# A first dense layer by seven block products for a pair of batches, in runs that use all PSUM banks

## The chip, the cores and the metric

The kernel runs on one core of one Trainium2 chip. The metric is device time in microseconds (us) of one execution; the time before is the median of three runs. A profile is one execution with the hardware profiler on; its span is the time from its first to its last instruction.

The engines: TensorE (PE) multiplies matrices and accumulates into the eight PSUM banks of 512 fp32 columns; PEld is its loading of weights, which overlaps matmuls. ScalarE (ACT) applies functions, VectorE (DVE) does arithmetic on whole tiles, GpSimd (POOL) and SyncE (SP) here only issue DMAs. Each engine works through its own queue in order and waits on semaphores for the others.

## The reference

There are 8 batches of 12 heads, 448 tokens and 64 dimensions a head, then a gated layer of width 2048:

```python
scores = q @ k.T / sqrt(64) - log(448)
attn = sigmoid(scores) @ v                  # per batch and head
x = attn, heads side by side                # 3584 tokens x 768
h = x @ w_in                                # 768 x 2048, first layer
g = h * sigmoid(beta * h)
out = g @ w_out                             # 2048 x 768, second layer
```

The kernel computes in fp16 with fp32 accumulation.

## The kernel before, in words

Four heads make a "quad" `g` (three quads a batch, 24 in all), two heads a slot. A **visit** (`visit`, L222) works on one quad and one chunk `jt` of 128 keys (the last chunk has 64, and is done for two quads at once): eight score matmuls of 448 columns with 32 rows each, four of which run side by side in TensorE (`score`, L201), into two score tiles of two PSUM banks each. ScalarE then makes a sigmoid of each tile (`weigh`, L212, 128x896). `attend` (L267) multiplies a quad's weights with the values, 16 matmuls of which at least two run side by side, into two banks; VectorE casts the result into `xT`, the first layer's input (L276).

The first layer (`dense1`, L285) is done by column blocks `dc` of 128 of the 2048: six matmuls of 128x128 by 448 columns into one bank (192 of half width for batch 0), then ScalarE's sigmoid (L293) and VectorE's product (L296) into `gt`. `gt` holds two batches, a window of seven tiles of 128 tokens.

The second layer multiplies tiles of `gt` by `w_out`. Tiles 0, 1, 2 and 27 are done plainly (`dense2`, L315: 32 matmuls of 384 columns, or the like in other widths). The 24 tiles between are done in pairs by seven block products in place of eight (`strassen`, L397: 7 x 8 matmuls of 384 columns for two tiles). Its sums of `gt` (`hidden_sum`, L386) and of `w_out` (`weight_sum`, L361, once) and its additions of results (L416, L419, L421) are done by VectorE, with one copy by ScalarE.

PSUM's eight banks are split: after the early stage two score tiles take four banks, and the other four (`bank`) serve values, first and second layer in turn, the one that was used longest ago first; a bank whose sum is still open is held (`held`).

The order of work is written out by the kernel. The first and second layer are units in a list (`filler_stream`, L467); after each visit the loop at L594 issues as many units as a budget in estimated us allows, so that TensorE has matmuls while ScalarE makes the sigmoids. A batch's first layer thus lies between visits of the next batches, unit by unit (`dense1` of six matmuls, `strassen` of four). What is left after the last visit (some 16 first-layer units and the last second-layer tiles) runs at the end. Queries, keys and values are loaded by POOL (L111, L132, L139), results are stored by SP (L450).

Of the kernel before, what the change touches and what calls it, by code (L numbers as in the profile page):

```python
# [13 lines left out]
def kernel(  # L14
# [27 lines left out]
    NHC = DM // P  # L42
    NDC = DFF // P
# [12 lines left out]
    qTp = ctx.enter_context(tc.tile_pool(name="qTp", bufs=4))  # L56
    kTp = ctx.enter_context(tc.tile_pool(name="kTp", bufs=4))
    attnp = ctx.enter_context(tc.tile_pool(name="attnp", bufs=12))
# [3 lines left out]
    outp = ctx.enter_context(tc.tile_pool(name="outp", bufs=4))  # L62
    psum = {}
    used = {}
    held = {}

    def share_psum(pools: ExitStack, n_sc: int, n_one: int):
        for name, bufs in (("sc", n_sc), ("one", 1)):
            psum[name] = pools.enter_context(
                tc.tile_pool(  # L70
                    name=f"ps_{name}{n_sc}",
                    bufs=bufs,
                    space=bass.MemoryType.PSUM,
                    reuse_waits="tile",
                )
            )
        used.clear()
        used.update((i, i - n_one) for i in range(n_one))
# [4 lines left out]

    def bank(name: str, cols: int = S, hold=None):
        i = min((i for i in used if i not in held.values()), key=used.get)
        touch(i)
        if hold is not None:
            held[hold] = i
        return psum["one"].tile([P, cols], FP32, tag=f"one{i}", name=name)

# [5 lines left out]
    w_in16 = const.tile([P, NHC, DFF], FP16, name="w_in16")  # L96
    w_out16 = const.tile([P, NDC, DM], FP16, name="w_out16")

# [66 lines left out]


# [25 lines left out]
    def score_tile():  # L195
        return psum["sc"].tile([P, 2, 512], FP32, tag="sco", name="sco")
# [13 lines left out]
    def weigh(sco, n: int):  # L210
        at = attnp.tile([P, 2, S], FP16, tag="attnT", name="attnT")
        nc.scalar.activation(  # L212
            out=at[:, :, 0:n],
            in_=sco[:, :, 0:n],
            func=AF.Sigmoid,
            bias=nlogs[:, 0:1],
            scale=MSCALE,
        )
        return at


    def visit(g: int, jt: int, also=()):  # L222
        if jt < JF:
            todo = [(score_tile(), [s]) for s in (2 * g, 2 * g + 1)]
        else:
            todo = [(score_tile(), [2 * h, 2 * h + 1]) for h in (g, *also)]
        for e in range(PAIR):
            for sco, slots in todo:
                for s in slots:
                    for hh in range(2):  # L230
                        score(sco, 0, s, jt, hh, e, 0, S)
        for sco, slots in todo:
            at = weigh(sco, S)
            for s in slots:
                at_tiles[s, jt, 0] = at


    def half_visit(g: int, c0: int, second: int):
# [14 lines left out]
        for s, jt, sco, u0 in plan:  # L253
            at_tiles[s, jt, c0] = ats[id(sco)][:, :, u0 : u0 + QH]

    def attend(g: int, c0: int, n: int, part=(0, 1)):
# [4 lines left out]
        avs = [bank("av_ps") for _ in slots]  # L261
        todo = [(s, av, jt) for s, av in zip(slots, avs) for jt in range(JF)]
        for s, av, jt in todo + [(s, av, JF) for s, av in zip(slots, avs)]:
            at = at_tiles.pop((s, jt, c0))
# [16 lines left out]
    def dense1(b: int, dc: int, c0: int = 0, n: int = S):  # L281
        off = (b % 2) * S + c0
        m1 = bank("m1_ps")
        for hc in range(NHC):
            nc.tensor.matmul(  # L285
                m1[:, 0:n],
                w_in16[:, hc, dc * P : (dc + 1) * P],
                xTs[b][:, hc, c0 : c0 + n],
                start=(hc == 0),
                stop=(hc == NHC - 1),  # L290
            )
        sg = sigp.tile([P, S], FP32, tag="sg", name="sg")
        nc.scalar.activation(  # L293
            out=sg[:, 0:n], in_=m1[:, 0:n], func=AF.Sigmoid, bias=0.0, scale=beta_sb[:, dc : dc + 1]
        )
        nc.vector.tensor_tensor(  # L296
            out=gt[:, dc, off : off + n], in0=m1[:, 0:n], in1=sg[:, 0:n], op=ALU.mult
# [3 lines left out]
    N2 = 4  # L301

# [4 lines left out]
    def dense2(t: int, half: int, part: int):  # L307
        last = t == NT - 1
        mid = 512 if last else HALF
        lo, hi = (0, mid) if half == 0 else (mid, DM)  # L310
        if part == 0:
            m2s[t, half] = bank("m2_ps", hi - lo, (t, half))
        m2 = m2s[t, half]
        for dc in range(part * NDC // N2, (part + 1) * NDC // N2):
            nc.tensor.matmul(  # L315
                m2,
                gt[:, dc, cols(t)],
                w_out16[:, dc, lo:hi],
                start=(dc == 0),
                stop=(dc == NDC - 1),  # L320
            )
        if part < N2 - 1:
            return
        release((t, half))
        if half == 0:
            osbs[t] = outp.tile([P, DM], FP32, tag="osb", name="osb")
        osb = osbs[t]
        nc.vector.tensor_copy(out=osb[:, lo:hi], in_=m2)  # L328
        if last:
            store(t, lo, hi)  # L330
        elif half == 1:
            store(t, 0, DM)

    NT = NTOK // P

    def cols(t: int):
        return slice(t % NTILE * P, (t % NTILE + 1) * P)

# [8 lines left out]
    ws = {  # L347
        name: const.tile([P, ND, HALF], FP16, name=f"w_{name}")
        for name in ("T1", "T3", "T4", "T6", "T7")
    }  # L350

    def weight_sum(name: str, part: int):
# [8 lines left out]
        nc.vector.tensor_tensor(out=ws[name][:, rows], in0=x[:, rows], in1=y[:, rows], op=op)  # L361

# [25 lines left out]
    def strassen(t: int, i: int, part: int):  # L388
        name, x, _, op, w = product(t, i)
        if part == 0 and i + 2 < NPROD:  # L390
            hidden_sum(t, i + 2)
        first = (t, name) not in m2s
        if first:
            m2s[t, name] = bank("m2_ps", HALF, (t, name))
        m2 = m2s[t, name]
        for dc in range(part * ND // 2, (part + 1) * ND // 2):
            nc.tensor.matmul(  # L397
                m2,
                (x if op is None else sums[t, i])[:, dc],
                w[:, dc],  # L400
                start=first and dc == 0,
                stop=(dc == ND - 1),
                skip_group_check=i >= 4,
            )
            first = False if dc else first
        if part == 0:
# [46 lines left out]
    M1_US, M1H_US, M2_US, LEAST_US = 1.13, 0.58, 2.6, 2.0  # L453


    def second_layer(tiles):
        for t in tiles:
            if t < 3 or t == NT - 1:
                for half in range(2):
                    for part in range(N2):  # L460
                        yield M2_US / N2, lambda a=(t, half, part): dense2(*a), False
            elif t % 2:
                for i in range(NPROD):
                    for part in range(2):
                        yield M2_US / 4, lambda a=(t, i, part): strassen(*a), i in (2, 3) or (i, part) == (4, 0)

    def filler_stream():  # L467
        for c0 in (0, QH):
            for dc in range(NDC):
                if c0 and dc == 10:  # L470
                    for part in range(N2):
                        yield M2_US / N2, 0, lambda part=part: dense2(0, 0, part), False
                yield M1H_US, 0, lambda dc=dc, c0=c0: dense1(0, dc, c0, QH), False
        for t, half in ((1, 0), (2, 0), (0, 1), (1, 1), (2, 1)):
            for part in range(N2):
                yield M2_US / N2, 0, lambda a=(t, half, part): dense2(*a), False
        for b in range(1, B):
            for dc in range(NDC):
                yield M1_US, QPB * (b + 1), lambda b=b, dc=dc: dense1(b, dc), False
            ends = [((x * S // P) - 1) // 2 * 2 + 1 for x in (b, b + 1)]  # L480
            for cost, unit, opens in second_layer(range(ends[0], NT if b == B - 1 else ends[1])):
                yield cost, 0, unit, opens

    fill = list(filler_stream())
    at_fill = [0]

    def fill_units(n: int):
        for _ in range(n):
            fill[at_fill[0]][2]()
# [3 lines left out]
    firsts = ctx.enter_context(ExitStack())  # L493
    share_psum(firsts, 3, 2)
    with tc.manual_schedule():
# [9 lines left out]
        idle = bank("idle_ps", 512)  # L505
# [49 lines left out]
        firsts.close()  # L555
        share_psum(ctx, 2, 4)
        fill_units(4)
        half_visit(1, QH, 1)
        attend(0, QH, QH)
        fill_units(3)  # L560
        half_visit(2, QH, 0)
        fill_units(4)
        half_visit(2, QH, 1)
        attend(1, QH, QH)
        fill_units(4)
        transpose(QPB, 0)
        fill_units(1)
        attend(QPB - 1, QH, QH)
        transpose(QPB, 1)
        fill_units(4)  # L570

        visits = [(QPB, jt, ()) for jt in range(JF + 1)]
        for g in range(QPB + 1, NQUAD, 2):
            visits += [(g, jt, ()) for jt in range(JF)] + [(g, JF, (g + 1,))]
            visits += [(g + 1, jt, ()) for jt in range(JF)]
        spread = [3 * M1H_US, 3 * M1H_US + M2_US / 2, M2_US / 2 + 3 * M1H_US, 3 * M1H_US]
        spread += [5 * M2_US / 7] * 7
        spread += [2.95] * (sum(g < 4 * QPB for g, _, _ in visits) - len(spread))

        total = sum(u[0] for u in fill[at_fill[0] :])  # L580
        tail = 16 * M1_US + 9.6 * M2_US
        rest = (total - sum(spread) - tail) / (len(visits) - len(spread))
        adds = {
            5: [("T4", 0)],
            6: [("T4", 1)],
            8: [("T3", 0)],
            9: [("T3", 1), ("T1", 0)],
            10: [("T1", 1), ("T6", 0)],
            11: [("T6", 1)],
            12: [("T7", 0)],  # L590
            13: [("T7", 1)],
        }
        budget, spent = 0.0, 0.0
        for i, (g, jt, also) in enumerate(visits):  # L594
            if jt == 0:
                if g > QPB:


# [62 lines left out]
```

## Time and profile before

| | before |
|---|---|
| median of 3 runs | 388.36 us (387.67 to 388.69) |
| span of the profiled execution | 386.3 us |
| TensorE busy | 98% of the span, 2991 matmuls |
| ScalarE busy, VectorE busy | 63%, 59% |
| granted TensorE clock | full in all 40 slices |
| first-layer matmuls of 448 columns (L285) | 672, 134.2 us |
| first-layer matmuls of 224 columns (L285) | 192, 20.3 us |
| second-layer matmuls by block products (L397) | 672, 119.5 us |
| sigmoids of scores (L212, 896 columns) | 165, 157.1 us |
| ScalarE idle, waiting for scores | 80.7 us |

The run's time is longer than the profiled span by about 2 us. Busy time of an engine is the union of its instructions' spans; a matmul's span (353 ns for 448 columns) is longer than the distance to the next one's start, since they are pipelined. A wait is put down to the instruction that ended last before it.

### The profile page before, as it was taken

Reading aid. Unit: us, or ns where it says so; the run is one execution under the profiler, and the core shown is the slowest. Engines: PE = TensorE matmul, PEld = TensorE weight load, DVE = VectorE, ACT = ScalarE, POOL = GpSimd, SP = SyncE. Lnnn points to the kernel's source line nnn. Section 1 sums busy time; section 2 is a strip of 40 time slices with the busy share of each in tenths; the row PEclk is TensorE's granted clock in tenths of the full one; section 3 lists DMA queues with packets and bytes.
Section 4 is the critical chain, followed back from the end, with each engine's and each line's share of the span. In section 5 each row is a group of like instructions: output and inputs, shape, how many; then the busy total and the mean of one; then the engine's idle time right before and its main releaser. Section 6 shows DMA issues by size and latency. Waiting matters only on the chain.

```text
span 386.3 us, 7378 instructions
## 1 busy us (share of the span) xinstructions
PE 379.8 (98%) x2991; PEld 191.4 (50%) x2991; DVE 229.5 (59%) x437; ACT 242.0 (63%) x329; POOL 67.4 (17%) x117
## 2 busy tenths in 40 slices
PE   8989999999999999999999999999999999999996
PEld 3468754444554444444554445544455444555563
DVE  3356465784766557555765566655586565645762
ACT  4987966687384795597375783567762777625200
POOL 8833433131110410140110410104100000000000
PEclk9999999999999999999999999999999999999999
DMA  8999999828352850655363561639203300030033
GB/s 119 180 195 203 198 204 197 174 38 88 49 119 68 127 68 0 130 69 52 49 129 79 83 73 20 129 78 125 41 9 83 83 1 2 0 83 0 2 81 122
DMA packets 42401, 34.30 MB, mean 89 GB/s; under 512 B 21872, under 2 KB 38784, under 8 KB 42368
## 3 DMA queue, kind: packets, MB, share of 16 engines
q0 software_dynamic: 36976, 22.81, 43.1%
q1 hardware_dynamic: 5392, 11.02, 11.1%
q8 instruction: 23, 0.38, 0.4%
q14 instruction: 10, 0.08, 0.1%
HBM read 45.62 MB, written 11.01 MB: 147 GB/s over the span
## 4 chain that ended last, share of the span: by engine, by line
PE 97%; ACT 1%; DVE 1%; issue 0%
PE m_ps L285 39%; PE m_ps L397 29%; PE sco L201 12%; PE av_ps L267 9%; PE m_ps L315 6%; PE idle_ps L509 2%; ACT attnT L212 1%; DVE qT L179 0%; ACT sg L293 0%; DVE gt L296 0%; DVE kT L187 0%; DVE osb L328 0%; DVE xT L276 0%; DVE still L503 0%
## 5 line engine op out<-in xcount | busy, mean ns | idle before, releaser
L212 ACT ACTIVATE attnT<-sco,nlogs 128x896 f16<-128x896 f32 (+1 forms) x171 | 160.3, 991 | 81.3 <-PE sco L201 80.7
L285 PE MATMUL m_ps<-xT,w_in 128*128 128x448 f16 (+1 forms) x864 | 154.5, 332 | 1.3 <-ACT attnT L212 1.2
L296 DVE TENSOR_TENSOR gt<-m_ps,sg 128x448 f16<-128x448 f32 (+1 forms) x144 | 80.0, 572 | 84.2 <-ACT sg L293 84.2
L285 PEld LDWEIGHTS <-w_in 128*128 128x128 f16 x864 | 80.8, 98 | 71.7 <-issue 16.6
L293 ACT ACTIVATE sg<-m_ps,beta_sb 128x448 f32<-128x448 f32 (+1 forms) x144 | 82.3, 595 | 32.0 <-PE m_ps L285 29.9
L397 PEld LDWEIGHTS <-sum 128*128 128x128 f16 x480 | 45.2, 98 | 36.4 <-issue 7.9
L201 PE MATMUL sco<-qT,kT 32*128 32x448 f16 (+3 forms) x864 | 51.9, 340 | 1.0 <-ACT attnT L212 0.6
L397 PE MATMUL m_ps<-w_T,sum 128*128 128x384 f16 x288 | 51.6, 327 | 0.0
L111 POOL DMA_DIRECT2D raw<-in_q_dram x27 | 14.9, 553 | 189.9 <-DVE kT L191 183.5
L416 DVE TENSOR_TENSOR osb<-m_ps,osb 128x384 f32<-128x384 f32 x60 | 33.3, 555 | 18.7 <-PE m_ps L397 16.9
L267 PE MATMUL av_ps<-attnT,v 128*64 128x448 f16 (+3 forms) x432 | 41.3, 340 | 0.0
L276 DVE CAST xT<-av_ps 128x448 f16<-128x448 f32 (+1 forms) x54 | 28.6, 567 | 19.0 <-PE av_ps L267 19.0
L386 DVE TENSOR_TENSOR sum<-gt 128x1024 f16<-128x1024 f16 x60 | 39.1, 678 | 0.1
L397 PE MATMUL m_ps<-w_T,gt 128*128 128x384 f16 x192 | 34.2, 326 | 0.0
L397 PE MATMUL m_ps<-w_out,sum 128*128 128x384 f16 x192 | 33.7, 326 | 0.0
L267 PEld LDWEIGHTS <-v 128*64 128x64 f16 (+1 forms) x432 | 18.9, 107 | 23.8 <-issue 16.1
L201 PEld LDWEIGHTS <-kT 32*128 32x128 f16 (+1 forms) x864 | 13.4, 96 | 28.6 <-issue 25.9
L397 PEld LDWEIGHTS <-gt 128*128 128x128 f16 x192 | 18.1, 98 | 14.7 <-issue 3.1
L315 PE MATMUL m_ps<-w_out,gt 128*128 128x384 f16 (+2 forms) x128 | 22.5, 327 | 0.0
L132 POOL DMA_DIRECT2D v<-in_v_dram x32 | 19.8, 641 | 7.6 <-DMA w_in<-in_moe_w_in_dram 5.8
L179 DVE STREAM_TRANSPOSE qT<-raw 128x448 f32<-128x448 f32 (+1 forms) x27 | 16.5, 616 | 3.7 <-DMA raw<-in_q_dram 3.7
L315 PEld LDWEIGHTS <-gt 128*128 128x128 f16 x128 | 11.9, 98 | 10.3 <-issue 3.1
(24 smaller groups left out, 97.0 us busy)
## 6 DMA issues: line engine op xcount, KB each, us to landing
out_dram<-osb SPq DMA_DIRECT2D x98, 96.0 KB, 1.9
raw<-in_k_dram POOLq DMA_DIRECT2D x24, 224.0 KB, 4.5
raw<-in_q_dram POOLq DMA_DIRECT2D x21, 224.0 KB, 3.7
v<-in_v_dram POOLq DMA_DIRECT2D x32, 144.0 KB, 6.1
w_in<-in_moe_w_in_dram POOLq DMA_DIRECT2D x8, 384.0 KB, 10.4
w_out<-in_moe_w_out_dram POOLq DMA_DIRECT2D x4, 768.0 KB, 14.0
v<-in_v_dram POOLq DMA_DIRECT2D x16, 48.0 KB, 6.1
out_dram<-osb SPq DMA_DIRECT2D x2, 384.0 KB, 2.3
```

Source lines behind the costliest of these rows:

```text
L132: nc.gpsimd.dma_start(out=vs[b][i * BLK : (i + 1) * BLK, :, 0:JF].rearrange("p h j d -> p h (j d)"), in_=rows[:, :, JF * i * D : JF * (i + ...
L201: nc.tensor.matmul(sco[base : base + nk, hh, u0 : u0 + n], kT[g][lo : lo + BLK, jt * P : jt * P + nk, e], qT[g][lo : lo + BLK, c0 : c0 + n ...
L212: nc.scalar.activation(out=at[:, :, 0:n], in_=sco[:, :, 0:n], func=AF.Sigmoid, bias=nlogs[:, 0:1], scale=MSCALE,)
L267: nc.tensor.matmul(av[hh * D : (hh + 1) * D, 0:n], vs[b][base : base + nk, 2 * (s % NPAIR) + hh, jt], at[base : base + nk, hh, 0:n], start ...
L276: nc.vector.tensor_copy(out=xTs[b][:, s % NPAIR, c0 : c0 + n], in_=av[:, 0:n])
L285: nc.tensor.matmul(m1[:, 0:n], w_in16[:, hc, dc * P : (dc + 1) * P], xTs[b][:, hc, c0 : c0 + n], start=(hc == 0), stop=(hc == NHC - 1),)
L293: nc.scalar.activation(out=sg[:, 0:n], in_=m1[:, 0:n], func=AF.Sigmoid, bias=0.0, scale=beta_sb[:, dc : dc + 1])
L296: nc.vector.tensor_tensor(out=gt[:, dc, off : off + n], in0=m1[:, 0:n], in1=sg[:, 0:n], op=ALU.mult)
L315: nc.tensor.matmul(m2, gt[:, dc, cols(t)], w_out16[:, dc, lo:hi], start=(dc == 0), stop=(dc == NDC - 1),)
L386: nc.vector.tensor_tensor(out=sums[t, i], in0=x, in1=y, op=op)
L397: nc.tensor.matmul(m2, (x if op is None else sums[t, i])[:, dc], w[:, dc], start=first and dc == 0, stop=(dc == ND - 1), skip_group_check= ...
L416: nc.vector.tensor_tensor(out=out, in0=in0, in1=in1, op=op)
```

## The change

The first layer of batches 2 to 7 is done for two batches at once. With the 768 inputs and the 2048 outputs cut in halves, the 2x2 blocks of `w_in` and the two batches' halves of `xT` make seven products with sums of blocks (Winograd's form) in place of eight. Sums of `w_in` (`in_sum`) are made once, differences of `xT` (`x_sums`) for each pair. The second layer's window of two batches has seven tiles: three pairs, and one tile by itself (`single`, with the same number of matmuls as a plain tile). Two sums of `w_out` and one of `w_in` now overwrite their operands.

These first layers run without attention between: `first_layer` closes the values that are due, gives up the score tiles so that `bank` has all eight banks, and calls `blocks`. A run has eight blocks and makes 168 matmuls; at its two ends it issues four second-layer matmuls three times (`other`). Partial results are carried in PSUM and in free slots of the attention weights' buffer (`scratch`). Runs stand after the first visit of quads 12 and 18 and after the last one. Between them lie visits, values and second-layer matmuls, now in units of one matmul, paced by what is left over the visits that are left. Values come after the first scores of the next quad, not ahead of them.

PSUM is one tile with banks by index, the attention weights one buffer of 14 slots; `qT`, `kT` have three buffers for four, the output tiles three for four.

```diff
-    qTp = ctx.enter_context(tc.tile_pool(name="qTp", bufs=4))
-    kTp = ctx.enter_context(tc.tile_pool(name="kTp", bufs=4))
-    attnp = ctx.enter_context(tc.tile_pool(name="attnp", bufs=12))
+    qTp = ctx.enter_context(tc.tile_pool(name="qTp", bufs=3))
+    kTp = ctx.enter_context(tc.tile_pool(name="kTp", bufs=3))
...
-    outp = ctx.enter_context(tc.tile_pool(name="outp", bufs=4))
+    outp = ctx.enter_context(tc.tile_pool(name="outp", bufs=3))
...
+    ps = psp.tile([P, 8, 512], FP32, name="ps")
...
+    def share_psum(sc: int, first: bool = False):
+
+        age = min(used.values()) - 1 if first else max(used.values())
+        while len(scored) > sc:
+            used.update((i, age) for i in scored.pop())
+        while len(scored) < sc:
+            free = [i for i in used if i not in held.values()]
+            scored.append(
+                min(
+                    ((i, i + 1) for i in free if i + 1 in free),
+                    key=lambda two: sorted((used[i] for i in two), reverse=True),
                 )
             )
...
+    def single(t: int, n: int, dc: int):
+
+        if (n, dc) == (0, 0):
+            sums[t, 0] = sump.tile([P, ND, P], FP16, tag="sum", name="sum")
+            nc.vector.tensor_tensor(out=sums[t, 0], in0=hid(t, 0), in1=hid(t, 1), op=ALU.add)
...
+        half, x, w = (
+            (1, hid(t, 0), B12),
+            (0, hid(t, 1), B21),
+            (1, both, B22),
+            (0, both, B11),
+        )[n]
...
+    def in_sum(name: str, part: int):
+        x, y, op = {
+            "S3": (A11, A21, ALU.subtract),
+            "S1": (A21, A22, ALU.add),
+            "S2": (A22, us["S3"], ALU.subtract),
+            "S4": (A12, us["S2"], ALU.subtract),
+        }[name]
...
+        yield lambda: minus(t1[:, c], y[:, c], x[:, c])
+        yield lambda: minus(t2[:, c], y[:, d], t1[:, c])
+        yield lambda: minus(t3[:, c], y[:, d], y[:, c])
+        yield lambda: minus(t4[:, c], x[:, d], t2[:, c])
+
+    def product1(b: int, i: int, n: int, out, start: bool):
+
+        x, y = xTs[b], xTs[b + 1]
+        t1, t2, t3, t4 = xs[b]
+        w, m = (
+            (A11, x[:, 0:KH]),
+            (A12, x[:, KH:]),
+            (us["S4"], y[:, KH:]),
+            (A22, t4),
+            (us["S1"], t1),
+            (us["S2"], t2),
+            (us["S3"], t3),
+        )[n - 1]
+        for c in range(KH):
+            nc.tensor.matmul(
+                out,
+                w[:, c, i * P : (i + 1) * P],
+                m[:, c],
+                start=(start and c == 0),
+                stop=(c == KH - 1),
+                skip_group_check=not start,
+            )
+
+    def gate(h, dc: int, b: int):
+        sg = sigp.tile([P, S], FP32, tag="sg", name="sg")
+        nc.scalar.activation(
+            out=sg, in_=h, func=AF.Sigmoid, bias=0.0, scale=beta_sb[:, dc : dc + 1]
+        )
+        return lambda: nc.vector.tensor_tensor(
+            out=gt[:, dc, b % 2 * S : b % 2 * S + S], in0=h, in1=sg, op=ALU.mult
+        )
+
+    def blocks(b: int, other):
+
+        kept = {}
+
+        def whole(key, i):
+            h = kept.pop((i, key))
+            if (i, key) in held:
+                touch(held.pop((i, key)))
+            half, second = {"A": (0, 0), "D": (0, 1), "B": (1, 0), "E": (1, 1)}[key]
+            return gate(h, i + half * NB1, b + second)
+
+        for i in range(NB1 + 1):
+            p5 = scratch(6 + i % 2, 1).bitcast(FP32)
+            if i < NB1:
+                B = kept[i, "B"] = bank(S, (i, "B"))
+                product1(b, i, 1, B, True)
+                A = kept[i, "A"] = bank(S, (i, "A"), S)
+                nc.scalar.copy(out=A, in_=B)
+                D = kept[i, "D"] = bank(S, (i, "D"))
+                product1(b, i, 5, D, True)
+                nc.scalar.copy(out=p5, in_=D)
+            if i:
+                product1(b, i - 1, 3, kept[i - 1, "D"], False)
+                late = whole("E", i - 1)
+            else:
+                other()
+            if i < NB1:
+                product1(b, i, 6, B, False)
+                nc.vector.tensor_tensor(out=D, in0=B, in1=p5, op=ALU.add)
+            if i:
+                late()
+                whole("D", i - 1)()
+            if i < NB1:
+                product1(b, i, 2, A, False)
+                whole("A", i)()
+            if i in (0, NB1):
+                other()
+            if i:
+                product1(b, i - 1, 4, kept[i - 1, "B"], False)
+            if i < NB1:
+                product1(b, i, 7, B, False)
+                E = kept[i, "E"] = scratch(8 + i % 2, 1).bitcast(FP32)
+                nc.vector.tensor_tensor(out=E, in0=B, in1=p5, op=ALU.add)
+            if i:
+                whole("B", i - 1)()
...
+    M1_US, M2_US = 0.148, 0.164
...
+    def window(w: int):
+        yield from pairs(w * NTILE, 3)
+        yield from alone((w + 1) * NTILE - 1)
...
+        AV_US = 1.3
...
+        def first_layer(b: int):
+            while due:
+                values(due.pop())
+            while soon:
+                soon.pop(0)()
+            fill_units(len(fill) - at_fill[0] - ND)
+            share_psum(0, True)
+            fill.extend(window(b // 2))
+            blocks(b, lambda: fill_units(ND // 2))
...
+            if n in turn_at:
+                first_layer(turn_at[n])
+                share_psum(2)
...
+            todo = left_us(L1B) if g < 2 * QPB else left_us(len(fill)) - (2.0 if g < 6 * QPB else 4.0)
+            pace = (todo + phase["values"] * AV_US) / phase["visits"]
+            phase["visits"] -= 1
+            owed = pace
+            if jt == 0 and g > QPB:
+                due.append(g - 1)
+            while due or (at_fill[0] < len(fill) and fill[at_fill[0]][0] / 2 < owed):
+                if due and (jt >= 1 or clear()):
+                    values(due.pop())
+                elif fill[at_fill[0]][0] / 2 < owed:
+                    spend()
+                else:
+                    break
...
+        due.append(NQUAD - 1)
+        first_layer(B - 2)
         fill_units(len(fill) - at_fill[0])
```

## The prediction

> **What bounds the kernel now.** I read the page's busy table, then its clock row, then the waits, the groups by shape, and a stretch of the timeline in the middle.
>
> ```profile
> PE 379.8 (98%) x2991; PEld 191.4 (50%) x2991; DVE 229.5 (59%) x437; ACT 242.0 (63%) x329; POOL 67.4 (17%) x117
> PEclk9999999999999999999999999999999999999999
> ```
>
> ```profile
> 105.00:340.00 235.00, 235.00 (x1774) 111.43 (x1770) 144.52 (x264) 154.02 (x201) 27.57 (x48) 1.00 0.40 67
> ```
>
> The second fence is the windows view: length, then PE, PEld, DVE, ACT, POOL busy, then the granted clock. From 105 to 340 us TensorE is never idle and its clock is full. So the time is the sum of TensorE's matmuls, and only a shorter sum, or a new wait of TensorE, moves it.
>
> ```profile
> PE m_ps L285 <- ACT attnT L212: 1.2, 1, 1.2
> PE sco L201 <- ACT attnT L212: 0.6, 2, 0.3
> ```
>
> These waits (us, times, longest) are nearly all that TensorE spends on other engines: no wait is left to remove, and any that the change adds is lost in full. Next, what the followers of a matmul cost (groups by shape; between the bars stand the busy us and the mean ns of one, behind them the idle time before):
>
> ```profile
> L212 ACT ACTIVATE attnT<-sco,nlogs 128x896 f16<-128x896 f32 x165 | 157.1, 1004 | 81.3 <-PE sco L201 80.7
> L293 ACT ACTIVATE sg<-m_ps,beta_sb 128x448 f32<-128x448 f32 x112 | 68.8, 635 | 28.3 <-PE m_ps L285 28.3
> L296 DVE TENSOR_TENSOR gt<-m_ps,sg 128x448 f16<-128x448 f32 x112 | 67.9, 624 | 72.0 <-ACT sg L293 72.0
> L419 ACT COPY osb<-m_ps 128x384 f32<-128x384 f32 x12 | 5.7, 478 | 15.5 <-PE m_ps L397 15.5
> ```
>
> And the rhythm of one score visit (timeline, TensorE's and ScalarE's own rows):
>
> ```profile
> 191.77 0.57 PE L201 MATMUL sco<-qT,kT 32*128 32x448 f16 x8
> 192.28 2.12 PE L397 MATMUL m_ps<-w_T,sum 128*128 128x384 f16 x12
> 194.34 0.57 PE L201 MATMUL sco<-qT,kT 32*128 32x448 f16 x8
> ```
>
> ```profile
> 192.38 1.90 ACT L212 ACTIVATE attnT<-sco,nlogs 128x896 f16<-128x896 f32 x2 [4.84 <-PE sco L201]
> 194.95 1.91 ACT L212 ACTIVATE attnT<-sco,nlogs 128x896 f16<-128x896 f32 x2 [0.66 <-PE sco L201]
> ```
>
> Scores start at 191.77, ScalarE starts 0.61 later and is done 2.51 after them. TensorE's next scores come at 2.57 (0.60 for the scores with both changes of tile shape, and 12 matmuls), when the second score buffer is just free. From the trace's single instructions: 448-column matmuls start 0.189 us apart, 384-column ones 0.1625; the follower starts 0.20 after the last matmul's slot ended; TensorE resumes 0.05 after ScalarE frees a bank. So **a visit shorter than 2.56 us makes TensorE wait for ScalarE**. Before, the shortest had 12 matmuls and just fitted.
>
> **The change part by part.** I counted TensorE's instructions between score groups in the changed kernel's order.
>
> *Fewer matmuls.* Before, batches 2 to 7 take 6 x 96 = 576 first-layer matmuls of 448 columns; after, 3 pairs x 8 blocks x 7 products x 3 = 504. That is 72 x 0.189 = 13.6 us less. The second layer has one pair of tiles fewer and two single tiles more: 11 x 56 + 6 x 32 = 808 for 800, +8 x 0.1625 = +1.3. Score and value matmuls, and their changes of tile shape, stay. Net **-12.3 us**, if TensorE stays busy.
>
> *The runs.* In one block, TensorE's work is 21 x 0.189 = 3.97 us. ScalarE has four sigmoids and two copies. The copies are not in the trace (448 columns, one of them PSUM to PSUM): between 0.478 (L419's 384 columns) and 0.635 (a sigmoid of 448); I take 0.53, L419 scaled by the sigmoid's slope from 224 to 448 columns (454 and 635 ns). Sum 4 x 0.614 (68.8/112) + 1.06 = 3.52. VectorE has three gates from PSUM, one from SBUF, and two adds with an fp32 result, none of the last three shown: between 0.555 (the output add of 384 columns) and 0.69 (the copy of 512 columns at L328); at 0.61 (67.9/112) six are 3.66. Both fit below 3.97, ScalarE with 0.45, VectorE with 0.31 to spare. Laid out by order: product 6 waits for the copy of product 1, which is done 0.35 early; product 4 waits for VectorE's E, 1.2 early; product 7 waits for D = B + p5, which starts 0.20 after product 6 and takes 0.62, and two products (1.14) lie between: 0.27 early. So the middle of a run costs nothing extra, but D's cover is thin: each further 0.1 us would cost 2.4 us over 24 blocks.
>
> *Ends of the runs.* In the last block nothing stands between the products. E(7) waits in VectorE's queue behind gate A(7), so product 4 waits some 0.3; then the next scores take the bank of D(7), whose gate stands behind two sigmoids and two gates on E and D: E ready 1.5 us after product 3's start, sigmoids to 2.7, gates to 3.3, where TensorE is there at 2.2. So 1.1 + 0.3 for runs one and two, 0.3 for run three (no scores after): **+3.1**, less 0.3 as back-to-back gates start 0.56 apart: +2.8. *Starts:* first product waits only for a score buffer that is long read; runs two and three begin right after the value matmuls, and VectorE's two casts (1.2) and three differences (some 2.1, by the 678 ns of `sum<-gt` for 1024 columns) delay D(0) by about 0.4: **+0.8**.
>
> *Between the runs.* The order has 11 second-layer matmuls a visit where no values stand: 0.60 + 11 x 0.1625 = 2.39 us, below 2.56. With values it is 2.50 (16 value matmuls, 3 others). A wait of 0.17 in one visit makes the next one start later and fit, so it is paid about every second time: over seven visits (two with values) I get 0.54 us. Such visits are 49 (8 + 21 + 20): 7 x 0.54 = **+3.8**. Bounds: 0, if ScalarE's gap closes, to 49 x 0.17 = 8.3.
>
> *Batch 1 among attention.* Twelve first-layer matmuls a visit make two sigmoids each: 2 x 0.90 + 2 x 0.57 + gaps = 2.9 for ScalarE against 0.60 + 12 x 0.189 = 2.87 for TensorE, with one sum of weights (0.93, the mean of `w_T<-w_out`) a visit on VectorE: **+0.7** (0 to 2). The eight new sums of `w_in` (7.5 us) otherwise lie beside TensorE's matmuls, as VectorE is busy for 59%; where that cover is thin is the place just priced.
>
> *Buffers and tail.* Three output buffers for four: in the tail ScalarE's copy waits for the store of the pair before (four issues of some 0.45 us and 1.9 to land), which meets the product that adds to its bank by about 0.2 us twice; the last copy has 384 columns for 256, 0.555 for 0.42: **+0.5**. Queries' and keys' loads go out in the visits as before, and TensorE waited for none from 105 us on. The first-layer unit after the early half visits takes a bank that no score holds, so the 1.2 us wait shown goes or shrinks: **-0.6** (0 to -1.2).
>
> Sum: -12.3 + 2.8 + 0.8 + 3.8 + 0.7 + 0.5 - 0.6 = **-4.3 us**. The profiled execution's span is 386.3 us, so 382.0 after; the median of the runs, 388.36, lies 2.1 above the span, so **384.0 us**.
>
> **Rivals.**
> 1. *The new waits are smaller* (TensorE's end of scores hides them, a visit's sigmoids overlap): -12.3 with 1 to 4 us lost, 376.5 to 380.5. For it: ScalarE is at 63%. Against: the shortest visits before just fitted. Chance 0.17.
> 2. *The runs are bound by VectorE or ScalarE*, the other side: the place is D = B + p5 and the six operations a block. It decides from a mean of 0.66 us per VectorE operation (3.97/6), and the whole change is slower once a block takes 0.18 us more (4.3/24), so 4.15 us, 0.69 each. At 4.25 us a block it gives 384.0 + 24 x 0.28 = 390.7. For it: adds that write fp32 to PSUM are unmeasured, and each waits on another engine. Against: shown rows lie at 0.56 to 0.63. Chance 0.15.
> 3. *The clock drops in the runs.* Row: the granted clock is 1.00 in each window, also in the first 40 us with 3 us of idle TensorE. A pause in a run would have to lower the clock; a tenth of 95 us of runs at half clock costs 9.5 us: 393.5. Chance 0.02. [...]
> 4. *The change saves nothing*, the runs' order leaving as much idle as they save: within 1 us of 388.4. Chance 0.06.
>
> The forecast (381 to 387) has 0.60. Eight in ten: 379.0 to 390.5. A measurement of this kernel can tell about 0.3% (1.2 us) from no change: faster 0.78, same 0.07, slower 0.15.
>
> **What would show it.** TensorE matmuls fewer by 64; no or few TensorE waits inside a run, three groups of 31.8 us each; waits of the score matmuls for ScalarE of about 0.17 us, dozens of them; one wait for VectorE of about 1 us after runs one and two; clock 1.00. Wrong would be: long waits of L465 for VectorE or ScalarE in every block, or score waits over 0.2 us a visit.

## The result and the profile after

| | before | after |
|---|---|---|
| median, four runs each on one chip | 388.46 us (387.67 to 388.69) | 385.18 us (385.02 to 385.57) |
| span of the profiled execution | 386.3 us | 383.4 us |
| ratio | | 0.9916, 95% interval 0.9896 to 0.9936 |

The change makes the kernel 3.3 us faster by the medians, where 4.4 was forecast (384.0 against 388.4). The busy table and the clock row of the page after:

```profile
PE 374.5 (98%) x2927; PEld 187.1 (49%) x2927; DVE 264.4 (69%) x507; ACT 268.4 (70%) x376; POOL 67.5 (18%) x117
PEclk9999999999999999999999999999999999999999
```

TensorE has 64 matmuls fewer, as counted, and its busy time fell by 5.3 us. It is still the bound: 98% busy at full clock. ScalarE gained 26 us of work and VectorE 35. The windows view over the same 235 us as before:

```profile
105.00:340.00 235.00, 233.47 (x1701) 110.89 (x1694) 173.53 (x324) 177.03 (x245) 26.56 (x46) 1.00 0.37 64
```

Before, TensorE was busy for the whole of it. Now 1.53 us are idle, and as will be seen, idle time is not all that it waits. The waits of TensorE (us in total, times, longest), without those that stood there before:

```profile
PE ps L222 <- DVE gt L479: 0.9, 1, 0.9
...
PE ps L222 <- ACT attns L236: 0.7, 3, 0.3
PE ps L563 <- DVE w_out L407: 0.5, 1, 0.5
PE ps L563 <- DVE sum L552: 0.4, 1, 0.4
PE ps L312 <- DVE gt L326: 0.3, 1, 0.3
PE ps L563 <- DVE xT L301: 0.3, 1, 0.3
```

No wait of the first layer (L465) is in the list: the runs are not stopped from inside. (The starts of their matmuls say the same: inside the blocks they are 0.19 to 0.20 us apart throughout.) The groups by shape give the prices that the trace of before could not show (busy us, mean ns of one, then the idle time before them):

```profile
L476 ACT ACTIVATE sg<-ps,beta_sb 128x448 f32<-128x448 f32 x72 | 45.1, 630 | 7.9 <-PE ps L465 3.8
...
L476 ACT ACTIVATE sg<-attns,beta_sb 128x448 f32<-128x448 f32 x24 | 16.1, 670 | 2.9 <-DVE attns L525 2.9
...
L511 DVE TENSOR_TENSOR ps<-ps,attns 128x448 f32<-128x448 f32 x24 | 15.2, 632 | 16.9 <-PE ps L465 15.4 <-ACT sg L476 1.5
...
L503 ACT COPY attns<-ps 128x448 f32<-128x448 f32 x24 | 12.8, 533 | 1.1
L500 ACT COPY ps<-ps 128x448 f32<-128x448 f32 x24 | 12.4, 517 | 16.9 <-PE ps L465 15.7 <-DVE osb L581 1.1
```

The copies, taken at 0.53 us, cost 0.517 and 0.533; VectorE's addition D = B + p5 (L511), taken at 0.62, costs 0.632. Next, a stretch from the middle of run one (timeline of after: start, us, engine, instruction, and in brackets the idle time before it):

```profile
147.79 1.30 PE L465 MATMUL ps<-xT,w_S 128*128 128x448 f16 x6
...
148.92 0.73 PE L465 MATMUL ps<-xT,w_in 128*128 128x448 f16 x3
...
149.19 0.63 DVE L511 TENSOR_TENSOR ps<-ps,attns 128x448 f32<-128x448 f32 x1 [0.69 <-PE ps L465]
149.49 0.73 PE L465 MATMUL ps<-attns,w_in 128*128 128x448 f16 x3
...
150.06 0.73 PE L465 MATMUL ps<-xT,w_S 128*128 128x448 f16 x3
```

The first row holds products 3 and 6, whose last slot ends at 148.92. D starts 0.27 later and ends at 149.82. Products 2 and 4 lie beside it, and product 7, which needs it, starts at 150.06, right behind product 4. The slots follow each other at 0.57 us a product, so nothing is lost; with the 0.05 us that TensorE takes to go on, D came 0.19 early.

The visits are where time is lost. TensorE's rows of a stretch after run one, and ScalarE's beside them:

```profile
193.40 1.79 PE L563 MATMUL ps<-w_T,sum 128*128 128x384 f16 x10
195.12 0.80 PE L222 MATMUL ps<-qT,kT 32*128 32x448 f16 x8
...
198.01 0.58 PE L222 MATMUL ps<-qT,kT 32*128 32x448 f16 x8
```

```profile
193.39 1.91 ACT L236 ACTIVATE attns<-ps,nlogs 128x896 f16<-128x896 f32 x2 [0.76 <-PE ps L222]
```

ScalarE's second sigmoid ends at 195.30. It read the banks that the third score matmul of the group at 195.12 writes, so this one starts at 195.35, where it would otherwise start with the first two. The group shows as 0.80 us long where it takes 0.57 undisturbed, as the one at 198.01: a wait that no idle time shows, since the group's first two matmuls are still running. I found it in the distances from one start to the next. There are 21 such waits of 0.13 to 0.23 us and some smaller ones, 4.1 us in all.

### The profile page after: what moved, and what is told of

It is laid out like the page before. It is cut to its first block, busy times and chain, and to the rows that moved or that the text cites. A ratio compares the mean times of both kernels' runs of the same rounds, so it can differ in the third digit from the quotient of the medians.

```text
span 383.4 us, 7441 instructions
## 1 busy us (share of the span) xinstructions
PE 374.5 (98%) x2927; PEld 187.1 (49%) x2927; DVE 264.4 (69%) x507; ACT 268.4 (70%) x376; POOL 67.5 (18%) x117
## 4 chain that ended last, share of the span: by engine, by line
PE 90%; DVE 5%; ACT 3%; issue 1%; ACTq 0%; DVEq 0%
PE ps L563 26%; PE ps L465 23%; PE ps L222 12%; PE ps L292 10%; PE ps L312 8%; PE ps L341 4%; PE ps L379 4%; PE ps L682 3%; ACT attns L236 2%; DVE gt L479 2%; DVE ps L511 1%; ACT sg L476 1%; ACT sg L323 1%; DVE gt L326 0%; DVE attns L525 0%
## 5 line engine op out<-in xcount | busy, mean ns | idle before, releaser
L236 ACT ACTIVATE attns<-ps,nlogs 128x896 f16<-128x896 f32 (+1 forms) x171 | 160.5, 991 | 48.1 <-PE ps L222 47.1
L222 PE MATMUL ps<-qT,kT 32*128 32x448 f16 (+3 forms) x864 | 56.6, 340 | 1.7 <-DVE gt L479 0.9
L476 ACT ACTIVATE sg<-ps,beta_sb 128x448 f32<-128x448 f32 x72 | 45.1, 630 | 7.9 <-PE ps L465 3.8
L465 PE MATMUL ps<-xT,w_S 128*128 128x448 f16 x216 | 48.7, 352 | 0.1
L465 PE MATMUL ps<-xT,w_in 128*128 128x448 f16 x216 | 48.7, 353 | 0.0
L563 PE MATMUL ps<-w_T,sum 128*128 128x384 f16 x264 | 48.7, 327 | 0.0
L479 DVE TENSOR_TENSOR gt<-ps,sg 128x448 f16<-128x448 f32 x72 | 42.4, 616 | 0.6 <-ACT sg L476 0.5
L312 PE MATMUL ps<-xT,w_in 128*128 128x224 f16 (+1 forms) x288 | 40.7, 291 | 1.3 <-ACT attns L236 0.8
L292 PE MATMUL ps<-attns,v 128*64 128x448 f16 (+3 forms) x432 | 41.3, 340 | 0.0
L465 PEld LDWEIGHTS <-w_in 128*128 128x128 f16 x288 | 28.0, 98 | 26.6 <-issue 1.1
L581 DVE TENSOR_TENSOR osb<-ps,osb 128x384 f32<-128x384 f32 x55 | 30.5, 554 | 15.1 <-PE ps L563 12.6
L563 PE MATMUL ps<-w_out,gt 128*128 128x384 f16 x176 | 33.7, 327 | 0.5 <-DVE w_out L407 0.5
L465 PEld LDWEIGHTS <-w_S 128*128 128x128 f16 x216 | 21.1, 98 | 19.9 <-issue 0.6
## 6 DMA issues: line engine op xcount, KB each, us to landing
w_in<-in_moe_w_in_dram POOLq DMA_DIRECT2D x8, 384.0 KB, 10.5
out_dram<-osb SPq DMA_DIRECT2D x2, 384.0 KB, 2.4
```

Of the source, the lines that this page charges most:

```text
L222: nc.tensor.matmul(sco[base : base + nk, hh, u0 : u0 + n], kT[g][lo : lo + BLK, jt * P : jt * P + nk, e], qT[g][lo : lo + BLK, c0 : c0 + n ...
L236: nc.scalar.activation(out=attns[:, slot, :, 0:n], in_=sco[:, :, 0:n], func=AF.Sigmoid, bias=nlogs[:, 0:1], scale=MSCALE,)
L292: nc.tensor.matmul(av[hh * D : (hh + 1) * D, 0:n], vs[b][base : base + nk, 2 * (s % NPAIR) + hh, jt], at[base : base + nk, hh, 0:n], start ...
L312: nc.tensor.matmul(m1, w_in16[:, hc, dc * P : (dc + 1) * P], xTs[b][:, hc, c0 : c0 + n], start=(hc == 0), stop=(hc == NHC - 1),)
L465: nc.tensor.matmul(out, w[:, c, i * P : (i + 1) * P], m[:, c], start=(start and c == 0), stop=(c == KH - 1), skip_group_check=not start,)
L476: nc.scalar.activation(out=sg, in_=h, func=AF.Sigmoid, bias=0.0, scale=beta_sb[:, dc : dc + 1])
```

## The experiments

"Waits" are, from here on, what the distances between starts of TensorE's matmuls exceed those of undisturbed ones (0.189 us for 448 columns, 0.1625 for 384, and so on). They sum to some 5.7 us before (4.3 of it in the first 43 us) and 14.3 after. The theory: the runs' inside costs nothing; the gain of 12.3 us is paid back at the runs' edges and, most of all, in visits that are now shorter than ScalarE's two sigmoids. The rival: the products' additions and copies are the price.

**control**, the changed kernel once more.

> The changed kernel once more, as a control beside the others: 385.2 us, within 0.6.

384.73 us (384.26 to 385.15), ratio 0.9902 (0.9888 to 0.9917). The same within the interval; the following is set beside it.

**half_sigmoid** leaves out half of the columns of the attention's sigmoids from quad 6 on.

```diff
-            slot = weigh(sco, S, places.get(g, ()))
+            slot = weigh(sco, S, places.get(g, ()), QH if g >= 2 * QPB else None)
...
+                nc.gpsimd.memset(scratch(6, 4).bitcast(FP32), 0.0)
```

> From quad 6 on the sigmoid of the scores is made of the first half of the columns only (0.63 us in place of 1.00 an instruction; the other half keeps older numbers, and the spare slots are cleared by GpSimd after a run). Theory (TensorE waits in the visits for score banks that ScalarE still reads, 4.1 us): these waits go, the runs stay as they are, 381.1 us. Rival (the waits in the visits come from VectorE or from the order of second-layer matmuls): 385 us, waits stay.

379.84 us (379.33 to 380.81), ratio 0.9778 (0.9756 to 0.9800): 4.9 us less than the control. The same visit in its timeline, TensorE and then ScalarE:

```profile
193.25 0.57 PE L222 MATMUL ps<-qT,kT 32*128 32x448 f16 x8
```

```profile
193.92 1.16 ACT L237 ACTIVATE attns<-ps,nlogs 128x448 f16<-128x448 f32 x2 [1.24 <-PE ps L222]
```

No score group is lengthened any more. The runs are as they were, and so is the wait of 1.3 us behind run one. This shows that the visits' waits are ScalarE's, and what they cost; it went a little further than the 381.1 expected, since the wait of 0.54 behind run two and that of the second layer at 103 us (0.69, read below) went with them.

**eight_products** puts plain matmuls into the runs: no block products, sums, copies or additions, all else of the new order kept.

```diff
+        for n in range(2 * NDC):
+            d, u = n % NDC, b + n // NDC
+            h = bank(S)
+            for hc in range(NHC):
+                nc.tensor.matmul(
+                    h,
+                    w_in16[:, hc, d * P : (d + 1) * P],
+                    xTs[u][:, hc],
...
+            gate(h, d, u)()
```

> The first layer of batches 2 to 7 in the same runs at the same places, but by plain matmuls (eight block products for seven, no sums of w_in or of x, no copies and additions). Theory (the block products cost nothing beside their matmuls; the new order alone loses what was found in waits): 72 x 0.189 = 13.6 us more, less some 0.5 of the waits at a run's start and 1 at its end: 397 to 398.8 us, that is slower than the kernel before. Rival (the products' copies, sums and additions take back a part inside the runs): below 395.

394.44 us (394.31 to 394.62), ratio 1.0153 (1.0138 to 1.0168), below the expected 397 to 398.8. The new order alone is thus 5.9 us slower than before (388.55 on this chip; 1.3 of it are the eight more second-layer matmuls), and the products win 9.7 of the 13.6 that their matmuls are worth. Of the missing 3.9, 3.7 are waits that go when the products go (13.9 to 10.2): at the end of runs one and two 1.6, product 4 and the starts 0.9, behind run three 0.7, the second layer at 103 us 0.5. The rival was right, then: I had put too little on the products' side; but none of it lies in the middle of a run. The scores behind run one start without a pause:

```profile
170.99 0.81 PE L534 MATMUL ps<-w_out,gt 128*128 128x384 f16 x4
171.73 0.57 PE L222 MATMUL ps<-qT,kT 32*128 32x448 f16 x8
```

**double_d** makes D twice.

```diff
                 nc.vector.tensor_tensor(out=D, in0=B, in1=p5, op=ALU.add)
+                nc.vector.tensor_tensor(out=D, in0=B, in1=p5, op=ALU.add)
```

> VectorE makes D = B + p5 twice in each block (0.63 us more, same result). Theory (VectorE has some 0.3 us a block to spare and D is ready 0.27 us before product 7 needs it): each block 0.3 to 0.4 longer, 24 x 0.35 = 8.4, 393 to 394 us, with waits of product 7 for D. Rival (the runs have ample cover): 385 to 386.

397.32 us (396.92 to 397.80), ratio 1.0227 (1.0212 to 1.0243): 12.6 us more, where 8.4 were expected. The waits and a stretch of the timeline:

```profile
PE ps L465 <- DVE ps L512: 8.6, 24, 0.7
```

```profile
151.05 0.63 DVE L512 TENSOR_TENSOR ps<-ps,attns 128x448 f32<-128x448 f32 x1
...
151.74 0.73 PE L465 MATMUL ps<-xT,w_S 128*128 128x448 f16 x3 [0.33 <-DVE ps L512]
```

The second addition starts 0.67 after the first (it waits for it) and product 7 starts 0.06 after its end, 0.49 behind its slot at 151.25. From the second block of a run on, each takes 4.46 us for 3.97 (21 blocks, 10.3 us); the first block of a run loses 0.41 to 0.67 (1.7 in all), and product 4 waits 0.18 longer at each run's end (0.5). The difference 0.67 − 0.49 = 0.18 is D's cover, which agrees with the 0.19 read above and not with the 0.27 of the prediction. VectorE is busy for 3.92 us of such a block, so it is not full: the chain through D sets the block's length.

**fill_after_run** sets eight second-layer matmuls between runs one and two and the scores after them. **sum_order** makes the sums of `w_out` before those of `w_in`. **pace** costs a quad's values at 1.8 us in place of 1.3, so that visits without values have 12 matmuls, and those with them one.

```diff
+                fill_units(8)
```

```diff
-        sums_todo = [(in_sum, n, p, 0) for n in ("S3", "S2", "S4") for p in range(2)]
-        sums_todo += [(weight_sum, n, p, 0) for n in ("T7", "T6", "T1") for p in range(2)]
+        sums_todo = [(weight_sum, n, p, 0) for n in ("T7", "T6", "T1") for p in range(2)]
...
+        sums_todo += [(in_sum, n, p, 0) for n in ("S3", "S2", "S4") for p in range(2)]
```

```diff
-        AV_US = 1.3
+        AV_US = 1.8
...
-            todo = left_us(L1B) if g < 2 * QPB else left_us(len(fill)) - (2.0 if g < 6 * QPB else 4.0)
+            todo = left_us(L1B) if g < 2 * QPB else left_us(len(fill)) - (1.4 if g < 6 * QPB else 3.4)
```

> After runs one and two, eight second-layer matmuls (1.3 us) stand between the run and the next scores, taken from the visits that follow. Theory (the scores there wait 1.3 and 0.5 us for the gate of D(7), with nothing else for TensorE to do): these waits go, the visits get shorter and wait a little more, 384.7 - 1.8 + 0.6 = 383.5 us. Rival (the wait only moves to the second-layer matmuls, which need gates too): 384.7.

> The sums of w_out are made ahead of those of w_in, so that the one which overwrites w_out (T3) is done some visits before the first matmul that reads it. Theory (TensorE waited 0.7 us there): 384.0 us, the wait of a second-layer matmul for the sum of w_out gone. Rival (the wait moves to the next VectorE result): 384.7.

> A quad's values are put at 1.8 us in the pacing (1.3 before; the trace shows 1.77 with the changes of tile shape), and less second-layer work is kept for the stretch ahead of a run, so that visits without values have 12 second-layer matmuls (11 before), those with values one. Theory (a visit under 2.56 us makes scores wait for ScalarE): waits fall from 4.1 to about 1.5 us, as visits with 12 take 2.55 us, and one wait of 0.2 is left behind each visit with values: 382.5 to 383.5 us. Rival (the waits come with the number of visits, whatever their length): 384.7.

| | us | ratio to before | waits that went | waits that came |
|---|---|---|---|---|
| fill_after_run | 387.95 (387.63 to 388.53) | 0.9989 (0.9980 to 0.9999) | end of run one 1.3 to 0.5 | visits 4.1 to 7.1, second layer behind values 0.9 |
| sum_order | 385.14 (384.32 to 385.51) | 0.9908 (0.9895 to 0.9921) | second layer for `w_out` 0.7 | 0.5 at 108 us, more score waits |
| pace | 384.50 (384.14 to 385.63) | 0.9902 (0.9887 to 0.9918) | after runs one and two 1.0 | before run one 1.0 |

fill_after_run missed by 4.5 us and taught the most. Its visits' rows of the timeline:

```profile
169.78 0.57 PE L222 MATMUL ps<-qT,kT 32*128 32x448 f16 x7 [0.16 <-DVE gt L479]
...
172.18 0.71 PE L222 MATMUL ps<-qT,kT 32*128 32x448 f16 x8
...
177.16 0.72 PE L222 MATMUL ps<-qT,kT 32*128 32x448 f16 x8
```

The matmuls were taken out of visits that ScalarE paces. A visit with one matmul less is not shorter, it waits more: the eight that were moved after each of the two runs, 2.6 us together, come back as 3.0 us of score waits. The rival was wrong too, and of the two waits that were to go only the first shrank (behind run two 0.54 and 0.53). In sum_order the waits from 100 us to run one add up to 2.0 us, as without the edit: the rival, that the wait only moves on, was right. In pace the visits without values do fit. After each of runs one and two, a wait of 0.21 to 0.22 is left behind each of five visits with values, which are now 2.34 us long, and three waits of 0.06 elsewhere (1.3 us). I had expected 1.5 us of them in all three stretches of visits and forgot that each has that many; and ahead of run one the matmuls were short.

**all_three** has these three edits together (with 2.4 and 4.2 us kept back in place of 1.4 and 3.4, for the moved matmuls).

> The three edits together (matmuls after a run, order of the sums, pacing). Theory, sum of the single effects with fewer matmuls left for the visits: 381.5 to 382.5 us. Rival (they take from one another): no better than the best single one.

385.02 us (384.54 to 385.40), ratio 0.9908 (0.9894 to 0.9921): no better than the single ones, as the rival had it.

**d_first** and **d_first_pace** take up the one wait that ScalarE's rhythm does not set. In the last block the gate of D goes ahead of that of E, as the next scores take D's bank; the second kernel has with it pace's order, but only after run one.

```diff
-                late = whole("E", i - 1)
+                last = i == NB1
+                late = whole("D" if last else "E", i - 1)
...
-                whole("D", i - 1)()
+                whole("E" if last else "D", i - 1)()
```

> In the last block of a run D's sigmoid and gate go ahead of E's; nothing else is moved. The theory: TensorE waits 1.3 us for the scores after run 1 because the bank of D(7) is freed by the last of two gates (E, then D) in ScalarE's and VectorE's queues, so the order of the two sets it. Without E ahead, D's gate ends about one sigmoid or gate (0.6) earlier, and E's has no bank to free: the wait falls from 1.3 to 0.5 or less, the 0.54 at the second visit after run 2 by up to its whole, the 0.70 after run 3 little changed: 383.3 to 384.0. The rival: the queues are simply full at the end of a run, E's operations come between D and the next exponentials, and the first scores' exponential or the second layer waits instead: 384.4 to 385.2, no change.

> The same, and with it the order of pace (12 matmuls in a visit without values, 1 with) in the visits after runs 1 and 2 alone, where it took waits of 0.4 and 0.1 us away, and not before run 1, where it added 0.5. The theory: the two act on different waits and add up: 0.6 to 1.2 less from the end of run 1 and some 0.5 from the visits: 382.7 to 383.5. The rival: whatever TensorE saves ahead of a visit, the visit's exponentials give back, since ScalarE's rhythm sets the length of the visits from there on, as in the tries before: 384.4 to 385.2.

383.73 us (383.18 to 383.96), ratio 0.9878 (0.9861 to 0.9895), and 382.83 us (382.61 to 383.56), ratio 0.9859 (0.9844 to 0.9874), the fastest of all. The end of run one, first in the trace of after, then in that of d_first:

```profile
168.55 0.37 PE L222 MATMUL ps<-qT,kT 32*128 32x448 f16 x1
...
169.84 0.57 PE L222 MATMUL ps<-qT,kT 32*128 32x448 f16 x7 [0.93 <-DVE gt L479]
```

```profile
168.40 0.97 PE L222 MATMUL ps<-qT,kT 32*128 32x448 f16 x8
169.30 1.96 PE L564 MATMUL ps<-w_out,gt 128*128 128x384 f16 x11
```

After, one score matmul goes out and the second waits until VectorE's last gate frees the bank; the second layer follows at 170.35, 1.80 after the group's start, where 0.51 is usual: 1.29 lost. In d_first it follows after 0.90: 0.39 lost. The wait behind run two falls from 0.54 to 0.18, that behind run three, which was expected to stay, from 0.70 to 0.34. That is 1.6 us, against 1.0 by the medians of d_first and control (of two chips) and 1.7 by the spans of after and d_first. So queue order, not the amount of work, set most of the runs' ends. The further 0.9 of d_first_pace is not as sure: its waits from 44 us on are only 0.4 less (7.7 for 8.1), and the two intervals overlap.

## Why the prediction was right, and where its terms were off

The direction, the bound and the place of most of the new waits held, and 384.0 is within 1.2 us of 385.18; that it came so close is in part luck, since two terms below have about the right size for the wrong reason. The terms, against what the distances in the trace show:

| term | predicted | measured |
|---|---|---|
| fewer matmuls | −12.3 | −12.3 by count |
| middle of the runs | 0 | 0 |
| ends of the runs | +2.8 | +2.3 |
| starts of the runs | +0.8 | +0.5 |
| visits that wait for ScalarE | +3.8 | +4.1 |
| batch 1 among attention | +0.7 | +1.1 |
| buffers and tail | +0.5 | +0.3 |
| early wait for a bank, start | −0.6 | +0.1 |
| behind run three | none | +0.7 |
| sum | −4.3 | −3.2 |

The spans differ by −2.9 and the medians by −3.3; some 0.3 us of the spans' difference has no row in this table.

*The runs.* From first to last first-layer matmul a run takes 33.7 to 33.9 us. Less the 12 second-layer matmuls between (1.95) these are the three groups of 31.8 us that were to show it. That the middle costs nothing was right, with less to spare than thought: D starts 0.27 behind product 6's slot, not 0.20, so the cover of D is 0.18 and not 0.27, although VectorE's six operations take less of a block than was put (3.28 us by busy time, not 3.66). Rival 2 put its point of decision as a mean over VectorE's operations; double_d shows a block lengthened by the chain through D alone, with VectorE not full.

*Ends and starts.* Product 4 waits 0.16 in each run (0.3 predicted), the scores 1.29 behind run one (1.1). Behind run two the first scores do not wait and the second visit's do, 0.54. The starts of runs two and three lose 0.24 each, run one nothing. What was overlooked is run three: the forecast priced only product 4's wait there, as no scores follow, but the second layer waits, first for the last gate in VectorE's queue (0.14) and then for a sum of `gt` that stands behind it (0.56). d_first halved it.

*The visits.* This term decided the sum, and half_sigmoid confirms it, 4.9 us for 4.1. That a wait lets the next visit fit is seen in the alternation above (0.80, 0.58). One input was off: a visit with values takes 2.67 us (values 1.27, with changes of tile shape of 0.28 and 0.31 around them), not 2.50, so the scores that follow such a visit do not wait; but the visit after it has 11 matmuls, and the scores that follow that one do. The chance of 0.17 for smaller waits (rival 1) needed ScalarE to have room, and 63% of the whole span was no evidence of that within a visit. (Its range was also a little off: 12.3 saved with 1 to 4 lost gives 377.1 to 380.1, not 376.5 to 380.5.)

*Batch 1.* The sum was nearly right for the wrong reason. The visits themselves fit. What waits is the second layer behind them, once for a sum of `w_out` and once for VectorE's cast of the values:

```profile
102.86 0.95 DVE L407 TENSOR_TENSOR w_out<-w_out 128x1536 f16<-128x1536 f16 x1
...
103.86 0.97 PE L563 MATMUL ps<-w_out,gt 128*128 128x384 f16 x5 [0.53 <-DVE w_out L407]
...
125.06 1.16 DVE L301 CAST xT<-ps 128x448 f16<-128x448 f32 x2 [2.90 <-PE ps L292]
125.13 0.10 PEld L563 LDWEIGHTS <-sum 128*128 128x128 f16 x1
...
125.73 0.32 PE L563 MATMUL ps<-w_out,sum 128*128 128x384 f16 x1 [0.28 <-DVE xT L301]
```

The first is 0.69 us by the distances. It belongs to VectorE's longer queue, which the prediction called hidden because VectorE was busy for 59%: eight_products, which makes no sums of `w_in`, has 0.23 in its place, and sum_order moved it and did not remove it. The second is 0.44 and has nothing to do with sums: the weights are loaded at 125.13, the matmul starts 0.05 after the first cast ends (125.68), and eight_products has the same wait of 0.45. It opens a new result, so the likely reason is that it takes the bank of the values; no run tests that.

*Tail and start.* Here, too, the size is right and the reason is not: TensorE waits for no buffer in the tail, so the two waits of 0.2 us did not come. From the start of the last matmul to the end it is 0.34 longer, of which the wider last copy takes 0.13 (557 ns for 424); the rest lies around that copy and in the store behind it. The wait for the early bank shrank from 1.2 to 0.8 us of idle time, but the start took it back (below). Rivals 3 and 4 did not come: the granted clock is 1.00 in every window of the runs, though they go through all eight banks, and 1.0 over the profiled execution of double_d, where TensorE waits in each of the 24 blocks (8.6 us in all). The half clock in the runs that rival 3's 393.5 us are worked out from was my assumption; no trace shows it there.

## What to carry to other kernels

A matmul saved counts in full only where the follower is not the pace: in a loop that shares a rhythm with another engine, count the shortest iteration against that engine's time, since what is taken out of it is paid again as a wait (in fill_after_run, 2.6 us of matmuls came back as 3.0 us). When a pipelined block ends, put first in the followers' queues what frees the bank that the next stage takes; here the order of two gates was worth 1.0 us by the medians, where moving work into the gap cost 3. A thin cover is measured by doubling the covered operation: the delay that the second one adds, less the loss, is the cover (0.67 − 0.49 = 0.18 us in double_d).

## What the runs showed of the hardware

*The slow start of TensorE varied.* The timelines of before and after begin with the same thirteen 512-column matmuls. These are the last ten, first before, then after:

```profile
2.45 4.00 PE L509 MATMUL idle_ps<-still 128*128 128x512 f16 x10
```

```profile
2.44 4.47 PE L682 MATMUL ps<-still 128*128 128x512 f16 x10
```

They start 0.427 us apart at first and 0.216 apart later. The slow part, from the first matmul at 1.19 us, ends at about 5.8 us before, at 7.0 after and at 4.7 in the control. The trace's own list of granted clocks begins at just these times (5.83, 7.01 and 4.66), at 1.00, and the clock row counts the time ahead of it as full, so its first 9 says nothing of the start; the row that rival 3 took for the first 40 us is a record only from 5.83 us on. The first scores start at 6.38 us before, 6.85 after and 5.82 in the control: up to 1 us of difference between two single profiles is chance. The slow part lasts 4.6 us before, 5.8 after and 3.5 in the control, and 3.0 to 5.9 in all twelve profiles; why its end varies no run shows.

*Sigmoids from SBUF took 40 ns longer.* In after, the sigmoid of 448 columns took 670 ns from SBUF (24 of them) and 630 from PSUM (72; L476, above).

*VectorE's operations started closer where none waited for the one before.* Two additions of 0.63 us started 0.67 apart where the second waits for the first (double_d), while independent gates of 0.62 started 0.53 to 0.56 apart (after).
